# Another order of TensorE's work on the first four tiles: transposes of tiles 2 and 3 ahead of FFN blocks

## The chip, the core and the metric

The kernel runs on one core of a Trainium2 chip. The time is the device time of one execution in microseconds (us); the time of a kernel is the median of several runs. The engines are TensorE (PE in the profile, with PEld for its weight loads), VectorE (DVE), ScalarE (ACT), GpSimd (POOL) and SyncE (SP, which here only issues DMAs). Each runs its own instructions in order and waits on semaphores for the others.

## The reference

Input x has 2048 rows (tokens) of 640 numbers in bf16. With `xn` the layer norm of x without weights, the kernel computes a linear attention with 32 heads of 20 and an FFN of width 1728 that gates it:

```python
xn = (x - mean) / sqrt(var + 1e-5)
q, k, v = split(xn @ wqkv)                      # 32 heads of 20
pq, pk = phi(q), phi(k)                         # t+1 above 0, exp(t) below, + 1e-6
o = (pq @ (pk^T v)) / (pq . sum(pk) + 1e-6)     # per head
s = o @ wo
g = silu(relu(xn @ w1) @ w2)
out = x + s * g
```

## The kernel before

The 2048 tokens are 16 tiles of 128; the 640 features are 5 blocks of 128. TensorE needs `xn` with the features on the partitions, in `xnT`. The other tiles get there by a transposing DMA of the normed tile (`xnT_dma`, line 462). The first four can't wait for that and go another way:

- `T_raw(t)` (line 432) transposes the raw tile t on TensorE, five blocks of 128x128, into PSUM bank 4 + t. ACT copies the result into `xnT` (line 441). For tile 1 alone the work is cut: ACT copies three blocks, and DVE two from bank 0 (line 445).
- `T_sum(t)` (line 449) multiplies the copied tile by a matrix of ones on TensorE, five matmuls, which leaves the sum over the features of each token on all partitions, in the same bank.
- `T_center(t)` (line 454) is one DVE instruction that subtracts sum / 640 from the tile in `xnT`, in place. The division by the deviation is left to the evictions behind later products.
- `H_first(t, f)` (line 586) is the FFN's first product for tile t alone and the block f of 128 hidden features (f = 0, 1, 2): five matmuls of 128x128 into a slice of bank 2, 3 or 4. It needs the centred tile t. Behind tile 3 the whole bank of 512 tokens is evicted by ACT (line 562).

Tile 0 goes through `T_first` (line 414), which subtracts the mean on DVE ahead of the transposes. `fill` (line 353) issues matmuls on constants that nothing reads. Behind the first three FFN blocks come `K_step` (line 658: the k product, line 472, for tiles 0 to 7) and `H_block` (line 565) for the other hidden features, with 512 tokens each.

The order of each engine's instructions is the order of the calls in the program: a list per engine is built while the Python code runs (`Sched`, line 21), and the waits are worked out from what each operation reads and writes. TensorE executes strictly in that order as far as waits go, so a block that waits holds up all behind it. The calls around the change are written out by hand in lines 591 to 623. DMAs are issued in their own order by SP: x tiles 0 to 3 first, then the k weights (held until tile 0 is centred), then the second part of w1 (line 360, held until `T_center(1)`), x tiles 4 to 7, the third part of w1 and the q weights. The first part of w1, which `H_first` reads, is issued by ACT at the start.

## Time and profile before

| | us |
|---|---|
| median of three runs (222.99, 223.00, 223.22) | 223.00 |
| the profiled execution | 223.15 |
| its span | 221.4 |
| TensorE busy (97% of the span) | 215.8 |
| VectorE busy | 114.6 |
| ScalarE busy | 86.1 |
| GpSimd busy | 43.7 |

A row of the timeline gives the start in us from the beginning of the span, the length, the engine, the line, the operation, what it writes and reads, the shape and the count of instructions merged into it; in brackets stands the idle time of the engine before it and what ended that. The ends of matmuls are modelled and overlap with the next one's start. A row of the chain of waits gives start, length and what ran. The rows of a table of stretches give the length and then, for each engine, its busy time with the count of instructions; then the clock granted to TensorE, the DMA share and the rate of transfer.

### The profile page before, as it was taken

The page shows a single profiled execution, that of the slowest core. Times are in us where ns is not written, and L with a number is a line of the kernel's source. Part 1 is how long each engine was busy: PE and PEld are TensorE (multiplying, and loading weights), DVE is VectorE, ACT ScalarE, POOL GpSimd, SP SyncE. Part 2 cuts the span into 40 slices and gives each one's busy share as a digit, 9 for nine tenths or more (in the row PEclk, how much of TensorE's full clock was granted, in tenths as well). Part 3 has the DMA queues.
Part 4 walks back from the last instruction along what each step waited for, and adds up shares of the span by engine and source line. Part 5 has one row for each costly group of instructions (what it writes and reads, how often), then busy time and mean ns, then how long its engine had stood idle before and what let it go on. Part 6 is the DMA issues. An engine that isn't in the chain of part 4 may idle for free.

```text
span 221.4 us, 3528 instructions
## 1 busy us (share of the span) xinstructions
PE 215.8 (97%) x1463; PEld 133.9 (60%) x1474; DVE 114.6 (52%) x193; ACT 86.1 (39%) x138; POOL 43.7 (20%) x66
## 2 busy tenths in 40 slices
PE   7999999999999999999999999999999999999994
PEld 2865554455545554444467778767767776776672
DVE  2687845889687999996710006603322222314063
ACT  2368665567656656555322114641021102110300
POOL 4053101259222998700000000000000000000001
PEclk9999999999999999999999999999999999999999
DMA  6899581211012105800059969369110101000002
GB/s 190 242 357 250 131 234 41 59 30 33 0 30 59 33 0 104 170 12 3 0 178 365 272 178 353 93 201 322 62 59 3 61 30 33 30 31 33 30 30 89
DMA packets 28156, 24.51 MB, mean 111 GB/s; under 512 B 11796, under 2 KB 27500, under 8 KB 28140
## 3 DMA queue, kind: packets, MB, share of 16 engines
q1 hardware_dynamic: 27484, 23.79, 36.7%
q10 hardware_dynamic: 656, 0.49, 0.8%
q8 instruction: 11, 0.18, 0.4%
q14 instruction: 5, 0.04, 0.1%
HBM read 15.75 MB, written 5.24 MB: 95 GB/s over the span
## 4 chain that ended last, share of the span: by engine, by line
PE 95%; DVE 1%; DMA 1%; issue 0%; ACT 0%
PE psT L841 26%; PE psT L555 25%; PE psT L472 10%; PE psT L786 10%; PE psT L540 10%; PE psT L887 10%; DMA reg<-in_A_x_dram 1%; PE psT L857 1%; PE psT L577 1%; PE psT L797 1%; PE psT L808 1%; PE psT L645 1%; PE psT L450 1%; DVE reg L902 0%; DVE stats L392 0%
## 5 line engine op out<-in xcount | busy, mean ns | idle before, releaser
L555 PE MATMUL psT<-reg 128*128 128x512 bf16 (+1 forms) x295 | 59.8, 346 | 0.7 <-issue 0.2
L841 PE MATMUL psT<-reg,hT 128*128 128x320 bf16 x416 | 60.1, 299 | 0.0
L841 PEld LDWEIGHTS psT<-reg,hT 128*128 128x128 bf16 x416 | 40.4, 98 | 16.4 <-issue 1.1
L555 PEld LDWEIGHTS psT<-reg 128*128 128x128 bf16 x305 | 27.3, 98 | 26.8 <-issue 0.4
L909 DVE TENSOR_TENSOR reg<-psT,reg 128x640 bf16<-128x640 f32 x15 | 12.4, 825 | 54.0 <-PE psT L887 53.9
L562 ACT ACTIVATE hT<-psT 128x512 bf16<-128x512 f32 x52 | 30.9, 598 | 18.2 <-PE psT L555 18.1
L875 ACT ACTIVATE reg<-psT 128x640 bf16<-128x640 f32 (+1 forms) x13 | 8.4, 661 | 44.3 <-PE psT L841 24.9
L894 POOL TENSOR_TENSOR reg<-reg 128x320 bf16<-128x320 bf16 x1 | 0.8, 788 | 124.6 <-DVE reg L902 124.6
L540 PE MATMUL psT<-reg 128*128 128x512 bf16 x99 | 24.6, 379 | 0.1
L472 PE MATMUL psT<-reg 128*128 128x320 bf16 x160 | 24.2, 299 | 0.0
L481 POOL TENSOR_TENSOR zacc<-zacc,reg 128x640 f32<-128x640 f32 x16 | 23.7, 1484 | 1.9 <-DVE reg L515 1.0
L887 PE MATMUL psT<-reg,pqT 128*128 128x320 bf16 (+2 forms) x165 | 24.0, 295 | 0.0
L786 PE MATMUL psT<-reg 128*128 128x320 bf16 x160 | 21.9, 299 | 0.0
L472 PEld LDWEIGHTS psT<-reg 128*128 128x128 bf16 x160 | 15.6, 98 | 8.2
L887 PEld LDWEIGHTS psT<-reg,pqT 128*128 128x128 bf16 x165 | 15.9, 98 | 6.0
L786 PEld LDWEIGHTS psT<-reg 128*128 128x128 bf16 x160 | 15.7, 98 | 6.2
L550 DVE SCALAR_TENSOR_TENSOR pqT<-er 128x512 bf16<-128x512 bf16 x20 | 17.1, 853 | 0.7
L540 PEld LDWEIGHTS psT<-reg 128*128 128x128 bf16 x100 | 9.7, 98 | 11.7 <-DVE er L548 0.6
L392 DVE BATCH_NORM_STATS2 stats<-reg 128x6 f32<-128x320 bf16 x32 | 14.0, 478 | 3.4 <-DMA reg<-in_A_x_dram 3.4
L547 ACT ACTIVATE er<-psT 128x512 bf16<-128x512 f32 x20 | 12.0, 598 | 8.9 <-PE psT L540 8.1
L548 DVE TENSOR_SCALAR er<-psT 128x512 bf16<-128x512 f32 x20 | 13.6, 679 | 3.1 <-ACT er L547 3.1
L515 DVE TENSOR_TENSOR reg<-ek 128x640 bf16<-128x640 bf16 x16 | 13.5, 843 | 1.5 <-ACT ek L506 1.0
(66 smaller groups left out, 134.6 us busy)
## 6 DMA issues: line engine op xcount, KB each, us to landing
reg<-in_A_x_dram SPq DMA_DIRECT2D x16, 160.0 KB, 4.1
rscr<-rden SPq DMA_DIRECT2D x4, 640.0 KB, 10.7
reg<-rscr SPq DMA_DIRECT2D x5, 512.0 KB, 6.1
reg<-in_A_x_dram SPq DMA_DIRECT2D x4, 640.0 KB, 6.2
out_dram<-reg SPq DMA_DIRECT2D x15, 160.0 KB, 1.8
reg<-in_A_wqkv_dram SPq DMA_DIRECT2D x2, 800.0 KB, 6.9
reg<-in_B_w_dram SPq DMA_DIRECT2D x1, 1120.0 KB, 5.9
reg<-in_B_w_dram SPq DMA_DIRECT2D x1, 1040.0 KB, 7.6
```

What stands on the lines that cost most here:

```text
L392: sc.op("DVE", lambda eng, a=a: eng.bn_stats(stats[:, t, a, :], xv[:, HN * a:HN * (a + 1)]), R=[("xin", t % XR)], W=[("stats", t, a)])
L472: fns.append(lambda eng, a=a, k=k: eng.matmul(ps[b + a][:, 0:HN], lhsT=xnT[:, k, tok(t)], rhs=wqk[:, k, D + HN * a:D + HN * (a + 1)], star ...
L481: sc.op("POOL", lambda eng: eng.tensor_tensor(out=zacc[:, :], in0=zacc[:, :], in1=pk[:, t, :], op=ALU.add), R=[("zacc",), ("pk", t)], W=[( ...
L515: sc.op("DVE", lambda eng: eng.tensor_tensor(out=pk[:, t, :], in0=e_, in1=r_, op=ALU.add), R=[("ek_e", es), ("ek_r", es)], W=[("pk", t)])
L540: sc.group("PE", [(lambda eng, k=k: eng.matmul(ps[b], lhsT=wqk[:, k, P * f:P * (f + 1)], rhs=rhs(k), start=(k == 0), stop=(k == C - 1))) f ...
L548: sc.op("DVE", lambda eng: eng.tensor_scalar(out=r_, in0=ps[b], scalar1=0.0, scalar2=1e-6, op0=ALU.max, op1=ALU.add), R=[("ps", b), ("er_e ...
L550: sc.op("DVE", lambda eng: eng.scalar_tensor_tensor(out=pqT[:, f, schunk(j)], in0=e_, scalar=1.0, in1=r_, op0=ALU.min, op1=ALU.add), R=[(" ...
L555: return sc.group("PE", [(lambda eng, k=k: eng.matmul(ps[b][:, lo:hi], lhsT=w1_sb[:, k, P * f:P * (f + 1)], rhs=xnT[:, k, 512 * j + lo:512 ...
L562: sc.op("ACT", lambda eng: eng.activation(out=hT[:, f, schunk(j)], in_=ps[b], func=ACTF.Relu), R=[("ps", b)], W=[("hT", j, f)])
L786: fns.append(lambda eng, t=t, a=a: eng.matmul(ps[b + a][:, 0:HN], lhsT=xn[:, t, P * k:P * (k + 1)], rhs=pk[:, t, HN * a:HN * (a + 1)], sta ...
L841: sc.group("PE", [(lambda eng, f=f, n=n: eng.matmul(ps[b + n][:, 0:HN], lhsT=hT[:, f, tok(t)], rhs=w2_sb[:, f, HN * n:HN * (n + 1)], start ...
L887: sc.group("PE", [(lambda eng, c=c, pb=pb, lo=lo, hi=hi: eng.matmul(ps[pb][:, 0:hi - lo], lhsT=pqT[:, c, tok(t)], rhs=wf[:, c, lo:hi], sta ...
```

## The change

Only calls change places. `T_raw(2)` moves from behind `T_center(1)` to right behind `H_first(0, 0)`, ahead of `T_sum(1)`. `T_raw(3)` moves to where `T_raw(2)` stood, so that it follows `T_sum(1)`. `H_first(0, 1)` moves from ahead of `T_sum(1)` to behind `T_raw(3)`, next to `H_first(0, 2)`. What is computed stays the same, as do the DMAs and their order.

```diff
     T_raw(1)
     H_first(0, 0)
-    H_first(0, 1)
+    T_raw(2)
     T_sum(1)
     held = [T_center(1)]
     w1_load(1, held)
...
     w_load(wqk[:, :, 0:D], A_wqkv[:, 0:D], ("wq",))
-    T_raw(2)
+    T_raw(3)
+    H_first(0, 1)
     H_first(0, 2)
-    T_raw(3)
     T_sum(2)
     T_center(2)
     H_first(1, 0)
```

TensorE's order from `T_raw(1)` to the group of FFN blocks is then, before and after:

```
before: T_raw1 H00 H01 T_sum1 T_raw2 H02 T_raw3 T_sum2 H10 T_sum3 H11 H12 H20 ...
after:  T_raw1 H00 T_raw2 T_sum1 T_raw3 H01 H02 T_sum2 H10 T_sum3 H11 H12 H20 ...
```

## The prediction

> **What bounds the kernel now.** I read the chain of waits first, on the page (its share by engine), then TensorE's timeline over the first 20 us, because the change touches nothing later.

> ```profile
> PE 95%; DVE 1%; DMA 1%; issue 0%; ACT 0%
> ```

> ```profile
> 0.82 3.57 PE L354 MATMUL psT<-const-bfloat16-1.0 128*128 128x512 bf16 x8 [0.82 <-PEq L986]
> 5.77 0.51 PE L438 MATMUL psT<-ident,reg 128*128 128x128 bf16 x5
> 6.12 0.72 PE L555 MATMUL psT<-reg 128*128 128x128 bf16 x10
> 6.85 0.44 PE L450 MATMUL psT<-reg,onesM 128*128 128x128 bf16 x5
> 7.12 0.44 PE L438 MATMUL psT<-ident,reg 128*128 128x128 bf16 x5
> 7.40 0.44 PE L555 MATMUL psT<-reg 128*128 128x128 bf16 x5
> 7.68 0.44 PE L438 MATMUL psT<-ident,reg 128*128 128x128 bf16 x5
> 8.36 0.45 PE L450 MATMUL psT<-reg,onesM 128*128 128x128 bf16 x5 [0.24 <-ACT reg L441]
> 8.65 0.44 PE L555 MATMUL psT<-reg 128*128 128x128 bf16 x5
> 8.96 0.45 PE L450 MATMUL psT<-reg,onesM 128*128 128x128 bf16 x5
> 9.24 2.40 PE L555 MATMUL psT<-reg 128*128 128x128 bf16 x40
> 11.48 2.88 PE L472 MATMUL psT<-reg 128*128 128x320 bf16 x20
> ```

> Columns: start, length, engine, line, operation, count, and in brackets the idle time before and what ended it. TensorE (PE) carries 95% of the chain, so time taken out of its row of work comes out of the kernel, as long as no other supplier takes the place. The group of 40 starts at 9.24 and the next group at 11.48: 2.24 / 40 = 56 ns from one 128-wide matmul to the next, 0.28 us for a block of five. The modelled ends overlap, so I count from start to start. The transposes at 7.68 should then free PE at 7.96, but T_sum(2) starts at 8.36: 0.40 us lost. T_sum(3) starts at 8.96 where 8.65 + 0.28 = 8.93 was possible: 0.03 more. As a check, from 7.96 to 9.24 are 1.28 us for three blocks (0.84): 0.44 us of holes. One hole stands earlier: the ten matmuls from 6.12 are through at 6.68, and T_sum(1) starts at 6.85 (0.17).

> What ends these holes is in the timelines of ACT and DVE for the same stretch:

> ```profile
> 6.21 0.49 ACT L441 ACTIVATE reg<-psT 128x384 bf16<-128x384 bf16 x1 [0.46 <-PE psT L438]
> 7.60 1.30 ACT L441 ACTIVATE reg<-psT 128x640 bf16<-128x640 bf16 x2 [0.90 <-PE psT L438]
> 8.20 0.70 ACT L441 ACTIVATE reg<-psT 128x640 bf16<-128x640 bf16 x1
> 6.32 0.29 DVE L445 COPY reg<-psT 128x256 bf16<-128x256 bf16 x1 [0.27 <-PE psT L438]
> 7.32 0.82 DVE L455 SCALAR_TENSOR_TENSOR reg<-psT,reg 128x640 bf16<-128x640 f32 x1 [0.71 <-PE psT L450]
> 8.85 1.56 DVE L455 SCALAR_TENSOR_TENSOR reg<-psT,reg 128x640 bf16<-128x640 f32 x2 [0.70 <-PE psT L450]
> 9.59 0.82 DVE L455 SCALAR_TENSOR_TENSOR reg<-psT,reg 128x640 bf16<-128x640 f32 x1
> ```

> ACT copies tile 2 out of PSUM from 7.60 to 8.30 (0.70; the row with x2 holds tiles 2 and 3, and tile 3 alone runs 8.20 to 8.90). T_sum(2) follows at 8.36, T_sum(3) at 8.96: 0.06 us after each copy. The holes are the latency transpose, copy, ones product; and ACT stands idle for 0.90 us just before 7.60, waiting for T_raw(2)'s transposes.

> **The change, part by part.** No instruction is added or removed; five-instruction blocks of 0.28 us change places. T_raw, T_sum and H_first issue no DMA, and no SP or POOL instruction changes place. The one SP instruction tied to this stretch is the second part of w1, held until T_center(1).

> T_raw(2) takes the place of H_first(0,1) ahead of T_sum(1). It starts at 6.12 + 0.28 = 6.40 instead of 7.12. T_sum(1) waits for tile 1's copies (ACT until 6.70, DVE until 6.61); the block before it is 0.28 us long either way, so the cover is the same, T_sum(1) stays at 6.85, T_center(1) at 7.32 to 8.14, and the SP queue behind it does not move. Cost nothing. The new wait is that T_raw(2) now stands in front of T_sum(1) on PE's in-order queue with its own need, tile 2 of x:

> ```profile
> L335 SPq DMA_DIRECT2D reg<-in_A_x_dram x1: 432/432/432, 1.7 to 1.7; - x1
> DMA to landing us min/median/max: 4.4/4.4/4.4
> ```

> Issued at 1.7 and 4.4 us to landing: 6.1, 0.3 before it is needed. Even a landing at 6.57 would cost nothing, since T_sum(1) has 0.17 us of slack of its own. The cost lies between nothing and the later landing; I take nothing.

> ACT's copy of tile 2 ran 0.48 us after the first transpose (7.12 to 7.60), so it now runs from 6.88 (ACT is free from 6.70) to 7.58. T_raw(3) follows T_sum(1) at 7.12 instead of 7.68, its copy runs from 7.60 to 8.30 instead of 8.20 to 8.90. H_first(0,1) and H_first(0,2) then stand at 7.40 and 7.68 and cover those copies. T_sum(2) could run from 7.58 + 0.06 = 7.64, so it starts when PE is free, at 7.96: the hole of 0.40 is gone. H_first(1,0) goes to 8.24 (it needs T_center(1), 8.14 + 0.06 = 8.20), T_sum(3) to 8.52 (needs 8.30 + 0.06 = 8.36): the hole of 0.03 is gone too. H_first(1,1) and (1,2) run to 9.36.

> What is late next is the centring on DVE. T_center(2) followed T_sum(2) by 0.49 (8.36 to 8.85): now 8.45 to 9.27. T_center(3) starts 0.74 behind it (8.85 to 9.59): 9.19 to 10.01. Tile 2's three FFN blocks want PE at 9.36 and can have it at 9.27 + 0.06 = 9.33; tile 3's want 9.36 + 3 x 0.28 = 10.20, can have 10.07. Margins of 0.03 to 0.13 us, thin but on the right side; if a centring were 0.1 late, PE would lose up to 0.07. Both ends: 0 and 0.1. I take 0, as each term is from a row of the same operation. K(0) then starts at 10.20 + 0.84 = 11.04 instead of 11.48: the sum is -0.44 us.

> Does PE stay the bound from 11.04 on? What is not tied to the moved blocks is the weights:

> ```profile
> 5.13 0.39 SPq L338 DMA_DIRECT2D reg<-in_A_wqkv_dram  x1
> reg<-in_A_wqkv_dram SPq DMA_DIRECT2D x1, 800.0 KB, 4.7
> 8.18 0.37 SPq L338 DMA_DIRECT2D reg<-in_B_w_dram  x1
> reg<-in_B_w_dram SPq DMA_DIRECT2D x1, 640.0 KB, 4.4
> 14.41 1.03 PE L555 MATMUL psT<-reg 128*128 128x512 bf16 x4
> 10.32 0.88 DVE L392 BATCH_NORM_STATS2 stats<-reg 128x6 f32<-128x320 bf16 x2
> ```

> The k weights land at 5.13 + 4.7 = 9.8 against a need at 11.04; w1's second part at 8.18 + 4.4 = 12.6 against 14.41 - 0.44 = 13.97. Both covers shrink by 0.44 and stay above 1.2 us. The statistics of tiles 1 to 3 on DVE stand behind T_center(3), which ends at 10.01 instead of 10.41: they come 0.4 earlier along with everything else. So the gain is kept to the end.

> The trace bears on the transposes' price too. In the grouping of PE's instructions by line and shape between 5.9 and 11.5:

> ```profile
> L555 PE MATMUL psT<-reg 128*128 128x128 bf16 x60 | 4.0, 219 | 0.0
> L438 PE MATMUL psT<-ident,reg 128*128 128x128 bf16 x15 | 1.4, 225 | 0.0
> ```

> A transpose lasts 225 ns against 219 ns for a matmul: moving one past the other changes no cadence. [...]

> **How it stands to the median.** The profiled execution took 223.15 us (span 221.4, so 1.75 around it); with 0.44 less, 222.7. The median of the three runs is 223.00, 0.15 lower. As the stretch concerned lies in front of everything, I take the same 0.44 off it: 222.56, put down as 222.55. That is 0.20% and so just at what a measurement of this kernel can tell from no change (0.2%, 0.45 us; the three runs spread over 0.23).

> **The rivals.**

> *The centring chain or tile 2's load eats part of the gain.* DVE's margins are 0.03 to 0.13 us. For it: nothing in this trace shows DVE centring tile 2 this close behind tile 1 (0.70 idle before 8.85, now 0.31). Against it: the two that did run back to back kept 0.74 spacing. If half the gain is lost: 223.00 - 0.22 = 222.78, no change that can be told. A late load belongs here and cannot turn the sign by much: at a landing of 7.07, where the old order is just not hit, the new T_sum(1) is 7.07 + 0.28 - 6.85 = 0.50 late, a net loss of 0.06, 223.06.

> *The change does nothing, because a transfer ends the stage.* If w1's second part landed at 14.4 rather than 12.6, H_block 3 would start where it does now: 223.0. Against it: 1.8 us of cover now, and PE has no idle time in front of 14.41 that a DMA ends.

> *Slower: TensorE's clock falls back.* PE's rows show two speeds, although the granted clock reads 1.00 in both stretches:

> ```profile
> 0.82:4.39 3.57, 3.56 (x8) 0.99 (x8) 0.93 (x3) 1.28 (x1) 1.22 (x5) 1.00 0.67 170
> 9.24:11.48 2.24, 2.24 (x44) 2.24 (x41) 2.21 (x6) 0.36 (x1) 0.00 (x0) 1.00 0.88 256
> 19.23 3.24 PE psT L555 x15
> L420 PE MATMUL psT<-ident,reg 128*128 128x128 bf16 x5 | 0.7, 304 | 0.5 <-DVE reg L415 0.5
> ```

> The first row is the eight 512-wide fills in 3.57 us, over 0.42 each; the third (of the chain) is fifteen 512-wide matmuls in 3.24, 0.216 each. Tile 0's transposes at 4.93 still take 304 ns; from 6.12 on the 128-wide matmuls are 56 ns apart. The new order puts ten transposes within 6.40 to 7.40, where the old one had five and an FFN block. If PE then ran one stretch like that of 9.24 to 11.48 at half rate, it would cost 2.24 us: 222.56 + 2.24 = 224.8. It decides from any fall that lasts over 0.9 us (half of which is 0.45 more than the gain of 0.44). Against it: the old order runs the same blocks with more idle time among them (0.44 us) and keeps the 56 ns throughout. [...]

> **How the numbers follow.** The full gain, 0.35 to 0.55 us: 0.72, split by the threshold into 0.50 faster and 0.22 within 0.2%. Half the gain or less lost: 0.12, within. A transfer that ends the stage: 0.03, within. The clock: 0.08, slower; a late load or a chain of waits that I have not seen and that costs over 0.45: 0.05, slower. Faster 0.50, same 0.37, slower 0.13. The range: low 222.30, where the hole of 0.17 before T_sum(1) goes too (222.39) and the median falls 0.1 lower; high 223.10, no change with half the runs' spread on top (0.1), which also holds the late load. Only the clock and the unseen wait lie outside. For faster or no change alone, 222.3 to 222.9.

> **What would show it.** T_raw(2) right behind 6.40 with ACT's copy near 6.9; T_sum(1) still at 6.85 and w1's second part still issued near 8.2; T_sum(2) near 7.96 with no idle time ended by ACT; K(0) at 11.04. Wrong would be: an idle time before T_raw(2) ended by the load of x, a hole before 9.36 or 10.20 ended by DVE L455, the spacing of 128-wide matmuls at twice 56 ns after 6.4, or a hole before the H_block at 13.97 that gives the 0.44 back.

## The result and the profile after

| | before | after |
|---|---|---|
| median, 19 runs of each | 223.08 us (222.85 to 223.45) | 222.62 us (222.33 to 222.90) |
| ratio | | 0.9978, 95% interval 0.9970 to 0.9985 |
| the profiled execution | 223.15 us | 222.90 us |
| its span | 221.4 us | 221.2 us |

The change takes 0.46 us off the median, 0.2%. The two profiled executions lie only 0.25 apart, which has to be explained too. TensorE's timeline of the changed kernel (start, length, line, operation, idle time before it in brackets, of which there is none here):

```profile
5.69 0.74 PE L438 MATMUL psT<-ident,reg 128*128 128x128 bf16 x5
6.22 0.69 PE L555 MATMUL psT<-reg 128*128 128x128 bf16 x5
6.75 0.44 PE L438 MATMUL psT<-ident,reg 128*128 128x128 bf16 x5
7.03 0.44 PE L450 MATMUL psT<-reg,onesM 128*128 128x128 bf16 x5
7.31 0.44 PE L438 MATMUL psT<-ident,reg 128*128 128x128 bf16 x5
7.59 0.72 PE L555 MATMUL psT<-reg 128*128 128x128 bf16 x10
8.15 0.44 PE L450 MATMUL psT<-reg,onesM 128*128 128x128 bf16 x5
8.43 0.44 PE L555 MATMUL psT<-reg 128*128 128x128 bf16 x5
8.71 0.44 PE L450 MATMUL psT<-reg,onesM 128*128 128x128 bf16 x5
8.98 2.40 PE L555 MATMUL psT<-reg 128*128 128x128 bf16 x40
11.22 2.88 PE L472 MATMUL psT<-reg 128*128 128x320 bf16 x20
```

From T_sum(1) at 7.03 on, every block starts 0.28 us behind the one before: the holes ahead of T_sum(2) and T_sum(3) are gone. From T_sum(1) to K(0) it takes 11.22 - 7.03 = 4.19 us, where before took 11.48 - 6.85 = 4.63: 0.44 less. But T_sum(1) itself is 0.18 later than before, so K(0) is only 0.26 earlier. The first two rows tell why: the blocks at 5.69 and 6.22 each take 0.53 us from start to start, those behind 0.28. In this execution TensorE reached its full rate near 6.7 us; in the profiled execution of before, T_raw(1) took 0.35 (5.77 to 6.12) and the block behind it the full rate's 0.28, so the rate had come up near 5.9. The trace's own records of the granted clock begin at just these moments, 6.73 and 5.91 us. That moment is no part of the change: until T_raw(2) starts at 6.75, TensorE's order is the same in both kernels.

ACT's copies and DVE's centrings of the same execution (tiles 2 and 3 on both rows):

```profile
7.23 1.30 ACT L441 ACTIVATE reg<-psT 128x640 bf16<-128x640 bf16 x2 [0.48 <-PE psT L438]
8.63 1.56 DVE L455 SCALAR_TENSOR_TENSOR reg<-psT,reg 128x640 bf16<-128x640 f32 x2 [0.29 <-PE psT L450]
```

The copies start 0.48 us behind T_raw(2) as before, and now end before the blocks between are done. ACT's idle time before them fell from 0.90 to 0.48, DVE's before tile 2's centring from 0.70 to 0.29.

### The profile page after: what moved, and what is told of

Read it like the earlier page. It is cut to its first block, busy times and chain, and to the rows that moved or that the text cites. A ratio compares the mean times of both kernels' runs of the same rounds, so it can differ in the third digit from the quotient of the medians.

```text
span 221.2 us, 3528 instructions
## 1 busy us (share of the span) xinstructions
PE 215.9 (98%) x1463; PEld 134.3 (61%) x1474; DVE 114.6 (52%) x193; ACT 86.1 (39%) x138; POOL 43.8 (20%) x66
## 4 chain that ended last, share of the span: by engine, by line
PE 96%; DVE 1%; DMA 1%; issue 0%
PE psT L841 26%; PE psT L555 25%; PE psT L786 10%; PE psT L472 10%; PE psT L540 10%; PE psT L887 10%; PE psT L857 1%; DMA reg<-in_A_x_dram 1%; PE psT L577 1%; PE psT L797 1%; PE psT L808 1%; PE psT L645 1%; PE psT L438 0%; DVE reg L902 0%; DVE stats L392 0%
## 5 line engine op out<-in xcount | busy, mean ns | idle before, releaser
L555 PE MATMUL psT<-reg 128*128 128x512 bf16 (+1 forms) x295 | 60.0, 348 | 0.7 <-issue 0.2
L555 PEld LDWEIGHTS psT<-reg 128*128 128x128 bf16 x305 | 27.6, 99 | 26.8 <-issue 0.4
L472 PE MATMUL psT<-reg 128*128 128x320 bf16 x160 | 24.2, 299 | 0.0
L472 PEld LDWEIGHTS psT<-reg 128*128 128x128 bf16 x160 | 15.6, 98 | 8.2
L392 DVE BATCH_NORM_STATS2 stats<-reg 128x6 f32<-128x320 bf16 x32 | 14.0, 479 | 3.3 <-DMA reg<-in_A_x_dram 3.3
## 6 DMA issues: line engine op xcount, KB each, us to landing
rscr<-rden SPq DMA_DIRECT2D x4, 640.0 KB, 10.6
```

What stands on the lines that cost most here:

```text
L392: sc.op("DVE", lambda eng, a=a: eng.bn_stats(stats[:, t, a, :], xv[:, HN * a:HN * (a + 1)]), R=[("xin", t % XR)], W=[("stats", t, a)])
L472: fns.append(lambda eng, a=a, k=k: eng.matmul(ps[b + a][:, 0:HN], lhsT=xnT[:, k, tok(t)], rhs=wqk[:, k, D + HN * a:D + HN * (a + 1)], star ...
L555: return sc.group("PE", [(lambda eng, k=k: eng.matmul(ps[b][:, lo:hi], lhsT=w1_sb[:, k, P * f:P * (f + 1)], rhs=xnT[:, k, 512 * j + lo:512 ...
```

## The experiments

Theory: TensorE is in order (before, H_first(1,0), whose centred tile is there at 8.14, stands until 8.65 behind T_sum(2), which waits until 8.36), and transposes, copy and ones product form a chain with a latency of their own (0.48, 0.70 and 0.06 us for tile 2); the change pays exactly as much as it covers of that latency. Rivals: one of the moved blocks does it alone; the moment of TensorE's speed-up does it, be it free or set by the transposes. "T_sum(1) to K(0)" below is read from start to start in the timeline of each profiled execution. Before has 4.63 us there, the changed kernel 4.19; both hold 15 blocks of 0.28 (4.2 us), and what is above that is holes.

**H_first(0,1) left in its place** (against the changed kernel):

```diff
     H_first(0, 0)
+    H_first(0, 1)
     T_raw(2)
...
     T_raw(3)
-    H_first(0, 1)
     H_first(0, 2)
```

> Both transposes moved up, H_first(0,1) left ahead of T_sum(1). Hole theory (the change pays because each transpose-copy-ones latency is covered by other blocks): T_sum(1) 0.11 later than in the fast case of before (6.96), holes of about 0.12 before T_sum(2) and 0.11 before H_first(1,0), from T_sum(1) to K(0) 4.15 us; in all -0.37 us against before. If H_first(0,1) in its new place carries most of the gain, the time is that of before.

Measured 222.66 against 223.08, ratio 0.9980 (0.9971 to 0.9989): -0.42 us. TensorE's timeline of this kernel:

```profile
6.64 0.44 PE L450 MATMUL psT<-reg,onesM 128*128 128x128 bf16 x5
6.92 0.44 PE L438 MATMUL psT<-ident,reg 128*128 128x128 bf16 x5
7.20 0.44 PE L555 MATMUL psT<-reg 128*128 128x128 bf16 x5
7.60 0.45 PE L450 MATMUL psT<-reg,onesM 128*128 128x128 bf16 x5
8.01 0.45 PE L555 MATMUL psT<-reg 128*128 128x128 bf16 x5
10.81 2.88 PE L472 MATMUL psT<-reg 128*128 128x320 bf16 x20
```

Both small holes are there: T_sum(2) at 7.60 where 7.48 was free (0.12), H_first(1,0) at 8.01 where 7.88 was free (0.13). T_sum(1) to K(0): 4.17, expected 4.15. Here that length holds only 14 blocks (3.92 us) and 0.25 of holes, since H_first(0,1) stands ahead of T_sum(1), so it can't be set against 4.63 and 4.19; the median can. The early transposes carry nearly the whole gain; whether H_first(0,1) moves too is worth less than these runs can tell.

**H_first(0,1) moved alone**, the transposes left behind T_center(1):

```diff
     H_first(0, 0)
-    T_raw(2)
     T_sum(1)
...
-    T_raw(3)
+    T_raw(2)
     H_first(0, 1)
     H_first(0, 2)
+    T_raw(3)
```

> Only H_first(0,1) moved, beside H_first(0,2); the transposes stay behind T_center(1). Hole theory: T_sum(1) loses its cover (a hole of about 0.45 before 6.85), holes of 0.12 before T_sum(2) and 0.28 before T_sum(3); from T_sum(1) to K(0) 4.87 us, the whole +0.24 us against before. If spreading the FFN blocks is what pays, it is faster than before.

Measured 223.28 against 223.08, ratio 1.0012 (1.0001 to 1.0024): +0.20 us where +0.24 was expected. Spreading the FFN blocks without the early transposes doesn't pay, and costs time by an interval that just leaves out no change. Its profiled execution was by far its slowest, 224.67 us. TensorE's timeline:

```profile
7.62 0.74 PE L438 MATMUL psT<-ident,reg 128*128 128x128 bf16 x5
8.15 1.25 PE L555 MATMUL psT<-reg 128*128 128x128 bf16 x10
9.22 0.47 PE L438 MATMUL psT<-ident,reg 128*128 128x128 bf16 x5
9.52 0.44 PE L450 MATMUL psT<-reg,onesM 128*128 128x128 bf16 x5
9.80 0.44 PE L555 MATMUL psT<-reg 128*128 128x128 bf16 x5
10.48 0.45 PE L450 MATMUL psT<-reg,onesM 128*128 128x128 bf16 x5 [0.24 <-ACT reg L441]
```

Until 9.2 a block takes 0.53 us, behind that 0.28: here TensorE stayed at half its rate some 3 us longer (5.9 and 6.7 in the profiles of before and of the changed kernel). So the length of T_sum(1) to K(0) can't be compared with the others; the median can. The part at the full rate still shows the hole before T_sum(3): it starts at 10.48, behind ACT's copy, where 10.08 was free. That is 0.40 us, the 0.12 and 0.28 expected before T_sum(2) and T_sum(3) taken together.

**No cover for the copies**: the changed order, with both FFN blocks moved on.

```diff
     T_raw(3)
-    H_first(0, 1)
-    H_first(0, 2)
     T_sum(2)
...
     T_center(3)
+    H_first(0, 1)
+    H_first(0, 2)
     H_first(1, 1)
```

> The changed order, but H_first(0,1) and (0,2) moved on behind T_sum(3), so that nothing covers tile 2's and tile 3's copies. Hole theory: holes of 0.24 before T_sum(2) and 0.28 before H_first(1,0) (it has to wait for T_center(1)); from T_sum(1) to K(0) 4.71 us against 4.19, time +0.52 us against the changed kernel, +0.08 against before. If the early transposes alone pay, it stays 0.4 under before.

Measured 223.17 against 223.08, ratio 1.0008 (0.9997 to 1.0019): +0.09, and 0.52 above the changed kernel on the same chip (222.65). TensorE's timeline:

```profile
6.72 0.44 PE L450 MATMUL psT<-reg,onesM 128*128 128x128 bf16 x5
7.00 0.44 PE L438 MATMUL psT<-ident,reg 128*128 128x128 bf16 x5
7.60 0.45 PE L450 MATMUL psT<-reg,onesM 128*128 128x128 bf16 x5 [0.16 <-ACT reg L441]
8.08 0.45 PE L555 MATMUL psT<-reg 128*128 128x128 bf16 x5
11.44 2.88 PE L472 MATMUL psT<-reg 128*128 128x320 bf16 x20
```

T_sum(2) waits for ACT again (7.28 was free, it starts at 7.60), H_first(1,0) for T_center(1) (7.88, starts at 8.08). T_sum(1) to K(0): 4.72, expected 4.71. So the early transposes pay only together with work to put behind them.

**The changed kernel again**, unaltered:

> The changed kernel unaltered, as the yardstick of this chip and as a second profile of when TensorE speeds up. Hole theory: from T_sum(1) to K(0) 4.19 us again whatever the speed before it, -0.44 us against before. Theory that the moment of the speed-up is free of the order of the blocks: the 128-wide matmuls go from 107 to 56 ns apart at another moment than 6.6 us. Rival, that the early transposes delay the speed-up: again near 6.6 us, as in the profile of the changed kernel, against 5.9 in the profile of before.

Measured 222.65 against 223.08, ratio 0.9983 (0.9975 to 0.9992): -0.43. Its timeline:

```profile
5.83 0.65 PE L438 MATMUL psT<-ident,reg 128*128 128x128 bf16 x5
6.31 0.44 PE L555 MATMUL psT<-reg 128*128 128x128 bf16 x5
7.00 0.44 PE L450 MATMUL psT<-reg,onesM 128*128 128x128 bf16 x5
11.18 2.88 PE L472 MATMUL psT<-reg 128*128 128x320 bf16 x20
```

T_sum(1) to K(0) is 4.18. Here H_first(0,0) runs at the full rate already (0.28, 6.31 to 6.59), and T_raw(1) takes 0.48 from start to start, between the 0.53 of half rate and 0.28, so the speed-up came during T_raw(1), ahead of 6.31 and not at 6.73: it isn't tied to this order. In the run without cover, which has T_raw(2) in the same early place, the 384-wide fill ahead of T_raw(1) takes 0.47 where it takes 0.53 in the profile of the changed kernel, and the row of T_raw(1) at 5.72 has the 0.44 us of a block at the full rate: there it had come by 5.72. The rival that the early transposes delay it falls, and already in the profile of the changed kernel the speed-up lay ahead of T_raw(2).

**Transposes in place of fills** (against the changed kernel), to see whether transposes count as work for TensorE's clock:

```diff
-    fill(8)
+    fill(2)
+    psf = ps[0].bitcast(bf)
+    sc.group("PE", [(lambda eng: eng.transpose(psf[:, 0:P], cones, ident[:])) for _ in range(25)], R=[("ident",)], W=[("ps", 0)])
```

> The changed kernel with six of the eight opening fills (512-wide matmuls on constants) replaced by 25 transposes of 128x128 over about the same stretch, 1.7 to 4.3 us. The rival of the prediction in which transposes do not count as work for TensorE's clock: the speed-up from 107 to 56 ns comes only some 3 us later than in the other profiles (4.9 to 6.6 us), and the time is 1 to 1.7 us above the changed kernel, 223.7 to 224.3. If transposes count like matmuls: speed-up between 4.9 and 6.6, time 222.6.

Measured 222.73 against 223.12, ratio 0.9980 (0.9961 to 0.9998). Its timeline:

```profile
1.71 2.57 PE L593 MATMUL psT<-ident,const-bfloat16-1.0 128*128 128x128 bf16 x25
4.84 0.57 PE L420 MATMUL psT<-ident,reg 128*128 128x128 bf16 x5 [0.56 <-DVE reg L415]
5.25 0.33 PE L354 MATMUL psT<-const-bfloat16-1.0 128*128 128x384 bf16 x1
```

and the durations of the 25 transposes (shortest, median, longest, in ns):

```profile
L593 PE MATMUL psT<-ident,const-bfloat16-1.0 x25: 219/314/314, 1.7 to 4.1; 128*128 128x128 bf16 x25
```

The 384-wide fill takes 0.33 us instead of the 0.53 of the profile of the changed kernel, and the last of the 25 transposes already take 219 ns, the length of a 128-wide matmul at the full rate. The full rate came during the transposes: at 107 ns from start to start at half rate and 56 at the full one, the 24 steps from 1.71 to 4.06 (the end of the row less 0.22) make an estimated 20 at half rate, so it came near 3.8 us, with two fills (0.83 to 1.71) and about 2.1 us of transposes ahead of it. The 12 executions took 222.54 to 223.40, none near 224. If transposes did not count, the stretch from 1.71 to 4.84 would be over 3 us of idle time, more than twice the 1.42 us of the run with six fills below, where ten of 12 executions took 223.65 to 224.57. In this run they did what the fills do.

**Without the 384-wide fill** between tile 0's and tile 1's transposes:

```diff
-    fill(1, 384)
     T_raw(1)
```

> The changed kernel without the 384-wide fill between tile 0's and tile 1's transposes. If that fill only takes room: T_raw(1) starts at the landing of its tile, up to 0.1 us sooner, time 222.5. If it is needed to keep TensorE's clock coming: the speed-up comes later in some executions, single times of 224 and more, median 0.1 to 0.4 above the changed kernel.

Measured 222.71 against 223.12, ratio 0.9980 (0.9954 to 1.0006). In the profiled execution T_raw(1) waits for its tile:

```profile
6.04 0.45 PE L438 MATMUL psT<-ident,reg 128*128 128x128 bf16 x5 [0.50 <-DMA reg<-in_A_x_dram]
```

The fill would have taken no room here; the landing of tile 1 sets T_raw(1). (In the profile of the changed kernel T_raw(1) stands right behind the fill, 0.32 us after its start at half rate; whether the fill holds it up there is not shown.) Two of its 12 executions took 224.23 and 224.42, such as the changed kernel did not show in its 30; too few to say that the fill prevents them, as before had three of 35 at 224.7 to 224.9 beside these runs.

**Nine and six opening fills instead of eight** (`fill(9)`, `fill(6)` in place of `fill(8)`, in the changed kernel):

> The changed kernel with nine opening fills instead of eight: the pause before tile 0's transposes shrinks from about 0.6 to about 0.2 us. Theory that the speed-up hangs on how busy TensorE was just before: it comes as early or earlier (4.5 to 6 us), never near 9, time 222.4 to 222.6 and a narrower spread. Theory that its moment is free of the work: 222.6 and the same spread.

> The changed kernel with six opening fills instead of eight: TensorE is idle from about 3.4 to 4.9 us. Theory that the speed-up hangs on how busy TensorE was just before: it comes some 3 us later in most executions, near 9 us, as in the profile of the kernel with H_first(0,1) moved alone, time 223.7 to 224.3. Theory that its moment is free of the work: 222.6.

With nine: 222.69 (222.50 to 222.95), ratio 0.9971 (0.9955 to 0.9988), neither faster nor narrower than the changed kernel (222.33 to 222.90). With six: 224.27, ratio 1.0028 (1.0004 to 1.0052); two of 12 executions stayed at 222.6, four took 223.65 to 224.18 and six 224.36 to 224.57. The busy times in short stretches of the one with six tell what happens (of the numbers at the end, the first is the granted clock):

```profile
6.60:6.80 0.20, 0.20 (x5) 0.08 (x2) 0.03 (x1) 0.12 (x1) 0.00 (x0) 1.00 0.67 70
6.80:7.00 0.20, 0.20 (x5) 0.17 (x4) 0.00 (x0) 0.10 (x1) 0.00 (x0) 0.89 0.37 83
7.00:7.20 0.20, 0.20 (x5) 0.20 (x4) 0.00 (x0) 0.20 (x1) 0.00 (x0) 0.50 0.69 205
9.00:10.00 1.00, 1.00 (x12) 1.00 (x11) 0.33 (x1) 0.00 (x0) 0.00 (x0) 0.50 0.65 83
10.20:10.40 0.20, 0.20 (x5) 0.20 (x4) 0.20 (x1) 0.00 (x0) 0.00 (x0) 0.58 1.02 215
10.40:10.60 0.20, 0.20 (x6) 0.20 (x5) 0.09 (x1) 0.00 (x0) 0.00 (x0) 1.00 0.90 241
```

and from TensorE's timeline of the same execution:

```profile
4.96 0.57 PE L420 MATMUL psT<-ident,reg 128*128 128x128 bf16 x5 [1.42 <-DVE reg L415]
```

I expected the clock to come late. It did not: tile 0's transposes take 0.57 us and the 384-wide fill behind them 0.33, against 0.73 and 0.53 in the profile of the changed kernel. Then it went back to half at about 6.96 (0.89 in the stretch from 6.8, that is 0.22 of it at half) and returned at about 10.37 (0.58: 0.84 of that stretch at half). The 3.4 us at half rate cost 1.7 us of work, and 224.36 for this execution against 222.65 for the profiled one with nine fills is 1.71. The one thing changed is two fills, and with them idle time well before the fall: 1.42 us ahead of tile 0's transposes against 0.45 in the profile of the changed kernel. I take that idle time for the cause; lengths in between were not tried, and two of 12 executions of the same program stayed at 222.6, so the idle time alone seems not to decide. Only one of the ten slow executions has a trace.

**The first part of w1 behind x tiles 1 or 2** (against the changed kernel; the second differs by one line):

```diff
-    for t in (1, 2, 3):
-        x_load(t)
-    dma("ACT", lambda eng: eng.dma_start(w1_sb[:, :, W1C[0]:W1C[1]], ...
+    x_load(1)
+    w1_load(0)
+    x_load(2)
+    x_load(3)
```

> The changed kernel with the first part of w1 issued by SP behind x tile 1, no longer by ACT beside tile 0. Theory that the start is now bound by the landing of tiles 0 and 1 (T_raw(1) waits for tile 1 until about 5.7 in the profiles with a fast clock): tile 0 and tile 1 land 0.4 us or more sooner, T_raw(1) starts near 5.2, K(0) near 10.6, time 222.1 to 222.4, another 0.3 to 0.5 below the changed kernel. Rival, that the moment of TensorE's speed-up binds the start: the earlier blocks only run slower, 222.6. If w1 comes too late for H_first(0,0), an idle time ended by its load appears, 222.7 or more.

> The same with the first part of w1 behind x tile 2. If tiles 0 and 1 bind: as with w1 behind tile 1, 222.1 to 222.4. If w1 is wanted first (by H_first(0,0)): 0.1 to 0.4 us later than with w1 behind tile 1.

Measured 223.17 and 223.41 against 223.12, ratios 0.9997 (0.9986 to 1.0009) and 1.0026 (1.0007 to 1.0045). TensorE's timeline with w1 behind tile 1:

```profile
5.16 0.44 PE L438 MATMUL psT<-ident,reg 128*128 128x128 bf16 x5
6.75 0.44 PE L555 MATMUL psT<-reg 128*128 128x128 bf16 x5 [1.15 <-DMA reg<-in_B_w_dram]
```

and behind tile 2:

```profile
7.04 0.44 PE L555 MATMUL psT<-reg 128*128 128x128 bf16 x5 [1.29 <-DMA reg<-in_B_w_dram]
```

T_raw(1) starts at 5.16 as hoped, and then H_first(0,0) waits 1.15 us for w1. Both loads are wanted at once; in these profiles putting one first only moves the wait. Two of the 11 executions with w1 behind tile 1 took 222.20 and 222.34, what was forecast where the landing of tiles 0 and 1 binds; they have no trace, and why they were faster is open.

**All of x first, and what needs no w1 first on TensorE**: loads x 1, 2, 3, then w1; TensorE's order T_raw 1, 2, 3, T_sum(1), T_sum(2), H_first(0,0), T_sum(3) and the other FFN blocks. The second kernel has a `fill(1, 384)` ahead of T_sum(2).

> An attempt at a faster version: x tiles 0 to 3 loaded ahead of the first part of w1, and what needs no w1 put first on TensorE (T_raw 1, 2, 3, T_sum(1), T_sum(2), then H_first(0,0), T_sum(3) and the other FFN blocks). If the landing of x and w1 binds the start and w1 lands near 7.0: T_raw(1) at 5.2, T_sum(2) near 6.9, the other blocks back to back, K(0) near 10.8, time 222.3 to 222.5, 0.2 to 0.3 below the changed kernel. If w1 lands 0.5 later, or if the pauses of 0.1 to 0.4 us before T_sum(1) and T_sum(2) bring TensorE's clock down: 223 and above, in single executions 224.

> The same with one 384-wide fill in the pause before T_sum(2). If only the landings bind: the same time as without the fill, within 0.1. If the pauses cost the clock: fewer executions of 224 and a lower median than without it.

Measured 223.07 and 222.96 against 222.98, ratios 1.0005 (0.9995 to 1.0015) and 0.9997 (0.9978 to 1.0015): the attempt gives the change's gain back. In the profiled execution with the fill, TensorE's timeline:

```profile
7.38 0.45 PE L555 MATMUL psT<-reg 128*128 128x128 bf16 x5 [0.33 <-DMA reg<-in_B_w_dram]
7.95 3.23 PE L555 MATMUL psT<-reg 128*128 128x128 bf16 x55
```

and the chain of waits (start, length, what ran):

```profile
4.71 6.51 DMA reg<-in_A_wqkv_dram
11.27 0.85 PE psT L472 x5
```

w1 lands at 7.4, and behind it the k weights (issued at 4.71) only at 11.2, where the prediction had them at 9.8: K(0) waits for them. Without the fill the chain passes through w1's second part, held until T_center(1) and 6.21 us on its way:

```profile
7.86 6.21 DMA reg<-in_B_w_dram
```

and TensorE waits for it (timeline):

```profile
14.34 1.03 PE L555 MATMUL psT<-reg 128*128 128x512 bf16 x4 [0.28 <-DMA reg<-in_B_w_dram]
```

No version that beats the changed kernel came out of this.

## Why the prediction was right, point by point

- **The sum, -0.44 us.** Measured -0.46 (0.33 to 0.67 by the interval), in the repeat -0.43; 222.62 against the forecast 222.55 (which stood on a median of 223.00; the later median of before is 223.08). In the profiles the holes come to 4.63 - 4.19 = 0.44. That the medians meet the sum within 0.02 is closer than the interval can promise, and partly luck.
- **The holes are uncovered latency, and the moved blocks cover it.** Shown by taking the cover away (T_sum(1) to K(0) 4.72) and by each part alone: with the early transposes alone -0.42, holes of 0.12 and 0.13 where they were expected; with H_first(0,1) moved alone +0.20.
- **T_sum(1) stays at 6.85, and w1's second part with it.** Wrong in the profiled execution: T_sum(1) at 7.03, T_raw(2) at 6.75 instead of 6.40, w1's second part issued at 8.36 instead of 8.18. The step took H_first(0,0) and T_raw(1) at the full rate, as in the one execution I had. The second profile has T_sum(1) at 7.00 and the one without cover at 6.72. TensorE's order up to there is the same in these three, and they differ in its speed-up (at 6.73, ahead of 6.31, by 5.72) and in the start of T_raw(1) (5.69, 5.83, 5.72); the difference does not belong to the change. The medians stand on 19 runs of each kernel, with different starts; that, by my estimate, is why a wrong start left the sum right. w1's second part still landed in time: no idle time ended by a load stands before the FFN blocks that read it.
- **No stall on tile 2's load.** T_raw(2) shows no idle time in front of it.
- **The centring chain on DVE holds its thin margins.** The group of 40 FFN matmuls runs 8.98 to 11.22 without a hole, 56 ns each; DVE's two centrings start 0.48 behind T_sum(2), against the 0.49 used.
- **The gain is kept behind K(0).** From K(0) to the end of the span 221.2 - 11.22 = 210.0, before 221.4 - 11.48 = 209.9.
- **A transpose costs what a matmul costs.** Right, and even closer than read: the 225 ns are a mean that holds the first transposes of T_raw(1), still at half rate (up to 291 ns). At the full rate both take 219.
- **The slower rival, the clock falling back,** did not come with this change. A fall did come in the profile with six fills (the granted clock at 0.50 from about 6.96 to 10.37; it cost 1.71 us, where the prediction put 2.24). That ten transposes close together would bring one about was the author's assumption, and no run shows it: with 25 transposes as fill TensorE came to its full rate during them, and the 12 executions took at most 223.40.

## What to carry to other kernels

Where an in-order engine runs short stages of several tiles, look at each idle time in its row, name the latency behind it, and put independent blocks between producer and consumer, as long as the ones moved away don't cover something else: moved alone, the same FFN block cost 0.20 us (0.02 to 0.54 by the interval). Measure such a change from one event to another inside the timeline (4.63 to 4.19), since the start shifted from one execution to the next (T_sum(1) at 6.72, 7.00 and 7.03 in three profiles with the same order up to there, 0.31 us, where the change is worth 0.46). When two loads are wanted at the same time, changing their order can just move the wait to the later one and to the loads behind it, as it did in these profiles (H_first(0,0) waited 1.15 and 1.29 us for w1, K(0) until 11.27 for the k weights).
